# Gated mix of grouped attention and a token-shift MLP: eleven products instead of twelve in the token mixing's w2, one product per group for the maxima, and query splits moved to GpSimd

## The chip, the cores and the metric

The kernel is one program on one core of a Trainium2 chip. The number that counts is the device time of one execution in microseconds (us); the median over several runs is given. The engines named below are PE (TensorE's matrix products; "PEld" is its loading of the stationary operand), DVE (VectorE), ACT (ScalarE), POOL (GpSimd), and SP, which here does nothing but issue transfers (DMAs). Each engine works through its own list of instructions in order, and an instruction that waits holds up all that is behind it on the same engine. The kernel schedules by hand: the order in which the Python code emits instructions is the order on each engine.

## The reference, cut to what matters

```python
x = A_x                                             # [1, 2048, 448]
g = sigmoid((x * gate_w).sum(-1, keepdims=True))
# a: 16 heads of 28, one shared key and value head
q = (x @ wq) per head; k = x @ wk; v = x @ wv
a = softmax(q k^T / sqrt(28)) v, heads joined, @ wo
# b: token mixing, then an MLP
h = gelu(layernorm(x) @ w1)                         # [2048, 448], four quarters of 112 channels
hs = concat(h0 shifted by +1, h1 by -1, h2 by +2, h3 by -2 tokens) @ w2
x1 = x + hs
b = x1 + gelu(layernorm(x1) @ w3) @ w4              # hidden width 1792
out = g * a + (1 - g) * b
```

All of it is float32. The kernel gets near float32 accuracy out of a faster, shorter format (`F32R`) by splitting each operand into a high and a low part, and by summing three products: high·high, high·low, low·high.

## The kernel before, in words

Tokens are worked on in four blocks of 512 (`NB`), each with four tiles of 128. A **unit** `u` is one block of queries with one group of four heads, so there are 16 units (`NU`), and `b, g = divmod(u, 4)`.

**Stage 1** makes queries, keys, values (`stage_q`, results to the DRAM buffer `qd`), and the token mixing. `stage_w1(b)` makes h for a block: for each quarter m (112 channels on partitions 0 to 111), eleven products, a multiplication by the layernorm factor on DVE (L410), two gelus on ACT giving the high part `hh[b]` and an unsplit copy (L411, L412), and the subtraction on POOL that leaves the low part `hl[b]` (L413). At its end POOL copies two columns between neighbouring blocks (L419, L420) or zeroes them (L417, L422). `stage_w2(b)` then needs for each of four tiles t and quarters m the products hh·w2h, hh·w2l and hl·w2h (L429 to L431): twelve products of 112 rows, 128 tokens, 448 columns, added into x1 by DVE (L433). The shift is a column offset in `hh`/`hl`. Rows 112 to 127 of `hh`, `hl`, `w2h` and `w2l` are unused.

The order is w1(0), w1(1), w2(0), w1(2), w2(1), four query products, w1(3), w2(2), w2(3). Between them the SP queue carries, in program order: the layernorm factors on their way through DRAM (`ln1_send` L371, `ln1_read` L376), `stage_kv` (L328, 16 rows of `qd` into `vT`, two transfers per block), `xt_write` (L166), and the loads for the MLP (`load_w34` L556, L557; `xt_read` L171, L173). After tile 0 of w2(2), `stage_v` transposes `vT` on PE (L349), and DVE copies the result out (L351, L352). So the PE's queue stands still there until `vT` of block 3 is loaded.

**Stage 2** is the MLP: for each block b, 14 steps f; a step has eleven products for w3 (`w3_part`, L130 to L134), two gelus (L634, L635), a DVE subtraction (`gl`, L636), and, two steps behind, twelve products for w4 (`w4_part`, L644 to L646). In between lie small jobs. One of them is the softmax's shift: for each unit, the maximum over the first 32 keys (`MK`) of each head's scores. The units 0 to 6 are done in block 2 at steps 2 to 8, the units 7 to 15 in block 3 at steps 0 to 8. In each such step: `max_cast` (DVE rounds the loaded queries into `qh0`, L620; then SP loads those of the next unit, L178), the w4 products, `max_all` (four products with 128 queries as the stationary and the keys `khd` as the moving operand, L203; DVE takes maxima straight out of PSUM, L204), and `max_end` (three small DVE operations, L223 to L227). `max_send` writes the result into `qd` in the next step: eight transfers, four issued by SP and four by ACT (L237).

**Stage 3** is attention: for every unit eight steps v, `k = 8u + v`. A step makes scores for two tiles of 128 keys (L820, four heads side by side on PE), exponentials on ACT (L830), where for head 3 DVE first copies the scores to SBUF (L828) and ACT works on the copy (L835), and then the products with the values of the step before (L845), added by DVE (L850). `q_begin(u)` splits a unit's loaded queries into high and low (`q_split`: L183, L184, on DVE). `q_begin(1)` and the fetch of unit 2 stand ahead of the loop; unit u + 2 follows at v = 6 of unit u.

Of the kernel before, what the change touches and what calls it, by code (L numbers as in the profile page):

```python
# [9 lines left out]
F32 = mybir.dt.float32  # L10
F32R = mybir.dt.float32r
AF = mybir.ActivationFunctionType
ALU = mybir.AluOpType
# [3 lines left out]
P = 128  # L17
# [19 lines left out]
def f32(ap):  # L37
    return ap.bitcast(F32)
# [3 lines left out]
def gated_mix_kernel(  # L42
# [134 lines left out]
        qr_of[u] = raw  # L177
        nc.sync.dma_start(raw, qd[g, :, 512 * b:512 * b + 512])  # L178

    def q_split(u, qh, ql):  # L180
        qr = qr_of.pop(u)
        qh_of[u], ql_of[u] = qh, ql
        nc.vector.tensor_copy(qh, qr)  # L183
        nc.vector.tensor_sub(ql, qr, f32(qh))  # L184

    def score(u, ps, j, keys, first=None, i=None):
        r = 32 * j
# [9 lines left out]
    def max_tile(name):  # L197
        return psA.tile([P, 512], F32, tag="mx", bufs=1, name=name)

    def max_all(u, ps):  # L200
        mx_of[u] = late.tile([P, 4, 4], F32, tag="mr", bufs=1, name=f"mr_{u}")
        for t in range(4):
            nc.tensor.matmul(ps[:, t * P:(t + 1) * P], qh_of[u][:, t * P:(t + 1) * P], khd, start=True, stop=True)  # L203
        nc.vector.reduce_max(mx_of[u].rearrange("p j t -> p t j"), ps.rearrange("p (t j k) -> p t j k", t=4, j=4), axis=AX.X)  # L204

    def max_full(u, tile_of):
        mr = s3.tile([P, 4, 4], F32, tag="mf", bufs=2, name=f"mf_{u}")
        for j in range(4):
            for t in range(4):
                mk = s3.tile([P, NB], F32, tag="mk", bufs=2, name=f"mk_{u}_{j}_{t}")  # L210
                for kb in range(NB):
                    ps = tile_of(f"mf_{u}_{j}_{t}_{kb}")
                    for n, rows, w, a in score(u, ps, j, slice(kb * 512, kb * 512 + 512), DH):
                        nc.tensor.matmul(ps, a[:, t * P:(t + 1) * P], w, start=(n == 0), stop=(n == 2),
                                         tile_position=(32 * j, 0))
                    nc.vector.reduce_max(mk[:, kb:kb + 1], ps, axis=AX.X)
                nc.vector.reduce_max(mr[:, j, t:t + 1], mk, axis=AX.X)
        mx_of[u] = mr

    def max_end(u, again=False):  # L220
        mr = mx_of.pop(u).rearrange("p j t -> p (j t)")
        mc = late.tile([P, 32], F32R, tag="mc", bufs=1, name=f"mc_{u}")
        nc.vector.tensor_scalar(mc[:, 0:16], mr, -1.0, None, op0=ALU.mult)  # L223
        nc.vector.scalar_tensor_tensor(mc[:, 16:32], mr, -1.0, f32(mc)[:, 0:16],
                                       op0=ALU.mult, op1=ALU.subtract)
        mrow = late.tile([P, 32], F32, tag="mrow", bufs=1, name=f"mrow_{u}")
        nc.vector.transpose(mrow, f32(mc))  # L227
        row_of[u] = mrow
        if again:
            max_send(u, f32(qh_of[u]), nc.sync)  # L230

    def max_send(u, q, other):
        mrow = row_of.pop(u)
        for k in range(2):
            for p in range(4):
                r = 32 * p + 16 * k
                (other if k else nc.sync).dma_start(  # L237
                    q[DH + k:P:32, :].rearrange("j (t p q) -> p j t q", p=4, q=32)[p], mrow[r:r + 16, :])

    ctx2 = ExitStack()  # L240

# [1 line left out]
    with tc.tile_pool(name="s1b", bufs=1) as s1b, \  # L243
# [156 lines left out]
        def stage_w1(b, between=None):  # L400
# [14 lines left out]
            for tt in (hh, hl):  # L415
# [5 lines left out]
                if b == NB - 1:  # L421
                    nc.gpsimd.memset(f32(tt[b])[0:C, :, 514:516], 0.0)  # L422

        def stage_w2(b, between=None):
            for t in range(4):
                ps = hs_tile(f"hs_{b}_{t}")[:, 0:D]
                for m in range(4):
                    o = 2 + t * P + SHIFTS[m]
                    nc.tensor.matmul(ps, hh[b][0:C, m, o:o + P], w2h[0:C, m, :], start=(m == 0), stop=False)  # L429
                    nc.tensor.matmul(ps, hh[b][0:C, m, o:o + P], w2l[0:C, m, :], start=False, stop=False)  # L430
                    nc.tensor.matmul(ps, hl[b][0:C, m, o:o + P], w2h[0:C, m, :], start=False, stop=(m == 3))  # L431
                xt = x1[:, 4 * b + t, :]
                nc.vector.tensor_add(xt, xt, ps)  # L433
                if between:
                    between(t)
# [56 lines left out]
                ln1_read(1)  # L492

        stage_w1(0, first)

        def second(m):
            if m < 2:
# [3 lines left out]
                ln1_tile(2, 2 * m - 3)  # L501

        stage_w1(1, second)
        stage_kv(0)
        stage_kv(1)

# [9 lines left out]
        ln1_tile(3, 3)  # L516
        mv0, rs0 = stats_tiles(s1, "m")
        stage_w1(2, lambda t: stats_tile(s1, 0, t, mv0))
        stats_end(mv0, rs0)
        ln1_send(3)  # L520
        ln1_read(3)
# [5 lines left out]
        for u in range(12, 16):  # L527
            stage_q(u)
        stage_w1(3)
        stage_kv(3)  # L530
        s1_stack.close()

# [75 lines left out]
    with tc.tile_pool(name="s2", bufs=1, reuse_waits="tile") as s2, \  # L608
# [3 lines left out]
                nc.gpsimd.tensor_scalar(x1[:, n, :], x1[:, n, :], gi[:, n:n + 1], None, op0=ALU.mult)  # L612

        def max_load(u):
            if u < NU:
                q_load(u, s2a.tile([P, 512], F32, tag="xn", bufs=1, name=f"qm_{u}"))

        def max_cast(u):
            qh_of[u] = qh0
            nc.vector.tensor_copy(qh0, qr_of.pop(u))  # L620
            max_load(u + 1) if u != 6 else None

        def w3_part(b, f):
            i, k = divmod(f, 2)
# [23 lines left out]
        for b in range(NB):  # L648
            acc = [ps2.tile([P, 512], F32, tag="acc", bufs=4, name=f"acc_{b}_{t}") for t in range(4)]
            gs = {}  # L650
            for f in range(NF):
                if f == 9 and b + 1 < NB:
                    mv, rs = layernorm_stats(s2a, b + 1)
                if f == 10 and b + 1 < NB:
                    xt4 = big(f"xt4_{b + 1}")[:, 0:4 * D].rearrange("p (f t j) -> p f t j", f=NE, t=4)
                if f in (10, 11) and b + 1 < NB:
                    for t in (2 * f - 20, 2 * f - 19):
                        xn = s2a.tile([P, 512], F32, tag="xn", bufs=1, name=f"xn_{b + 1}_{t}")[:, 0:D]
                        layernorm_norm(b + 1, t, mv, rs, xn, xt4)
                if f == 11 and b + 1 < NB:  # L660
                    xt_write(b + 1, xt4)
                    ln_read(b + 1)
                gs[f] = w3_part(b, f)
                if b == 0 and f % 2 and f < 11:
                    split_w3((f + 3) // 2)
                    split_w4((f + 3) // 2)
                    if f < 9:
                        load_w34((f + 5) // 2, s2a if f == 1 else s2)
                if b == 1 and f == 0:
                    nc.gpsimd.tensor_tensor(gg, invE, gz, ALU.pow)  # L670
                    nc.vector.tensor_scalar(gg, gg, 1.0, None, op0=ALU.add)
                    nc.vector.reciprocal(gg, gg)
                    nc.vector.tensor_scalar(gi, gg, -1.0, 1.0, op0=ALU.mult, op1=ALU.add)
                if b == NB - 1 and f == 4:
                    weigh_x1(0, 4 * b)
                if b == 1 and f in (0, 2, 4, 6):
                    load_k(f // 2, s2a.tile([P, 512], F32, tag="xn", bufs=1, name=f"kf_{f // 2}"))
                if b == 1 and f in (1, 3, 5, 7):
                    split_k(f // 2)
                if b == 2 and f == 1:  # L680
                    nc.gpsimd.memset(f32(khd), 0.0)
                    for j in range(4):
                        nc.sync.dma_start(f32(khd)[32 * j:32 * j + DH, j, :], f32(kH)[0:DH, 0:MK])
                    max_load(0)
                u = f - 2 if b == 2 and 2 <= f <= 8 else f + 7 if b == 3 and f <= 8 else None
                if b == 2 and f == 12:
                    max_load(7)
                if row_of:
                    w, = row_of
                    max_send(w, qd[w % NG, :, w // NG * 512:w // NG * 512 + 512], nc.scalar)  # L690
                if u is not None:
                    max_cast(u)
                if b == NB - 1 and f == 11:
                    q_load(0, s2a.tile([P, 512], F32, tag="xn", bufs=1, name="qr_0"))
                if b == NB - 1 and f == 13:
                    q_split(0, qh0, ql0)
                if f >= 2:
                    for t in range(4):
                        w4_part(f - 2, t, gs[f - 2], acc)
                if u is not None:  # L700
                    max_all(u, max_tile(f"m_{u}") if u % 2 else misc_tile(f"m_{u}"))
                    max_end(u)
            for t in range(4):
                w4_part(NF - 2, t, gs[NF - 2], acc, NF - 2 if b == NB - 1 else NF - 1)
                if b + 1 < NB:
# [11 lines left out]
    with tc.tile_pool(name="s3", bufs=1, reuse_waits="tile") as s3, \  # L717
# [18 lines left out]

        def q_begin(u):
            q_split(u, s3.tile([P, 512], F32R, tag="qh", bufs=3, name=f"qh_{u}"),
                    s3.tile([P, 512], F32R, tag="ql", bufs=3, name=f"ql_{u}"))

        q_fetch(1)
        q_begin(1)
        q_fetch(2)

        on_of = {}

# [112 lines left out]

        for k in range(NU * NV):  # L860
            u, v = divmod(k, NV)
            if v == 6 and u + 2 < NU:
                q_begin(u + 2)
                q_fetch(u + 3)
# [106 lines left out]
        with tc.If(again > 0, label="redo"):  # L971
            for b in range(NB):
                for g in range(NG):
# [1 line left out]
                    q_fetch(u)  # L975
                    q_begin(u)
                    max_full(u, bank)
                    max_end(u, True)
                    pv = take()
                    for kt in range(NT):  # L980
                        for j in range(4):
# [64 lines left out]
```

## Time and profile before

| | us |
|---|---|
| median of 3 runs (956.57 to 958.59) | 956.84 |
| the profiled execution | 957.32 |
| its span in the trace | 955.5 |
| PE busy | 928.2 |
| ACT busy | 645.6 |
| DVE busy | 549.2 |
| POOL busy | 74.5 |

Stage 1 fills the span up to 128.65 us, the MLP up to some 420 us, attention the rest. The shares of busy time are means over these stages, so what a change is worth has to be read from the stage in which it lies. In rows of the timeline the columns are start, duration (of the merged run of x instructions), engine, line, operation, tile, and in brackets the engine's idle time before it with what ended it. "SPq" rows are the issuing of transfers, not the transfers. In rows of windows, each engine has its busy time and count, and behind them stands the clock that PE was granted (1.00 is full), the share of the DMA engines' time, and GB/s.

### The profile page before, as it was taken

How to read it: one execution, taken by the hardware profiler on the slowest of the kernel's cores; microseconds unless marked ns; L12 is line 12 of the kernel's file. 1: busy time of each engine (PE TensorE's matmuls, PEld its weight loads, DVE VectorE, ACT ScalarE, POOL GpSimd, SP SyncE). 2: the span in 40 equal slices, each digit the busy share in tenths (PEclk: the TensorE clock that was granted, in tenths of full speed). 3: DMA queues.
4: the chain of work that ended last, by engine and by line, in shares of the span. 5: the costliest groups of instructions: out<-in, count | busy, mean ns of one | idle time of the engine just before them, and what ended most of it. 6: DMA issues, size and time to landing. Idle time of an engine off the chain costs nothing. (4 is left out here: it accounts for less than half of the span.)

```text
span 955.5 us, 24595 instructions
## 1 busy us (share of the span) xinstructions
PE 928.2 (97%) x10099; PEld 651.6 (68%) x10099; DVE 549.2 (57%) x1095; ACT 645.6 (68%) x1262; POOL 74.5 (8%) x105
## 2 busy tenths in 40 slices
PE   9999999999999989979999999999999999999996
PEld 6788888888888868865555555555555555555553
DVE  4664254532444544336667776776777767776674
ACT  5442444232321221138999999999999999999994
POOL 2232200221000520020000000000000000000000
PEclk9999999999999989989999999999999999999999
DMA  9802452210311311110000001100010000010001
GB/s 305 283 29 50 131 165 84 70 38 14 90 28 48 79 39 48 36 60 3 25 14 24 14 25 43 34 14 25 14 45 33 25 14 24 24 54 2 14 14 43
DMA packets 41079, 50.75 MB, mean 53 GB/s; under 512 B 9136, under 2 KB 27264, under 8 KB 40960
## 3 DMA queue, kind: packets, MB, share of 16 engines
q1 hardware_dynamic: 36656, 43.52, 15.6%
q10 hardware_dynamic: 4304, 5.61, 1.7%
q8 instruction: 80, 1.31, 0.6%
q14 instruction: 39, 0.32, 0.1%
HBM read 37.04 MB, written 11.93 MB: 51 GB/s over the span
## 5 line engine op out<-in xcount | busy, mean ns | idle before, releaser
L830 ACT ACTIVATE p<-bank 128x512 f32<-128x512 f32 x768 | 391.4, 628 | 9.1 <-PE bank L820 7.4
L845 PE MATMUL bank<-p,vext 128*32 128x256 f32 x4096 | 247.0, 382 | 2.1 <-ACT p L830 1.7
L828 DVE COPY p<-bank 128x512 f32<-128x512 f32 x256 | 175.1, 690 | 45.5 <-PE bank L820 44.7
L845 PEld LDWEIGHTS bank<-p,vext 128*32 128x32 f32 x4096 | 131.1, 110 | 91.9 <-DVE p L828 6.9
L634 ACT ACTIVATE gh<-g 128x512 fp32r<-128x512 f32 x55 | 32.8, 597 | 204.0 <-PE g L134 199.6
L835 ACT ACTIVATE p<-p 128x512 f32<-128x512 f32 x256 | 154.2, 687 | 3.4 <-DVE p L828 3.4
L850 DVE TENSOR_TENSOR o<-o,bank 128x256 f32<-128x256 f32 x222 | 93.5, 421 | 93.1 <-PE bank L845 49.2
L820 PE MATMUL bank<-qh,kH 30*128 30x512 f32 x1024 | 119.0, 445 | 5.3 <-DVE p L828 5.3
L636 DVE TENSOR_TENSOR gl<-gf,gh 128x512 fp32r<-128x512 f32 x55 | 38.6, 702 | 134.4 <-ACT gf L635 134.4
L820 PE MATMUL bank<-qh,kL 28*128 28x512 f32 x1024 | 106.1, 393 | 0.0
L820 PE MATMUL bank<-ql,kH 28*128 28x512 f32 x1024 | 105.4, 390 | 0.0
L820 PEld LDWEIGHTS bank<-qh,kH 30*128 30x128 f32 x1024 | 60.9, 183 | 63.4 <-ACT p L830 51.8
L645 PE MATMUL acc<-w4l,gh 128*128 128x448 f32 x220 | 80.4, 366 | 0.0
L644 PE MATMUL acc<-w4h,gh 128*128 128x448 f32 x220 | 80.3, 365 | 0.0
L646 PE MATMUL acc<-w4h,gl 128*128 128x448 f32 x220 | 80.2, 365 | 0.0
L782 PE MATMUL bank<-wof,on 128*32 128x224 f32 (+1 forms) x992 | 73.1, 370 | 5.2 <-ACT p L830 0.4
L130 PE MATMUL g<-ah,w3h 128*128 128x512 f32 x168 | 67.8, 403 | 0.0
L131 PE MATMUL g<-al,w3h 128*128 128x512 f32 x168 | 66.8, 397 | 0.0
L132 PE MATMUL g<-ah,w3l 128*128 128x512 f32 x168 | 66.4, 395 | 0.0
L782 PEld LDWEIGHTS bank<-wof,on 128*32 128x32 f32 x992 | 20.0, 108 | 56.7 <-ACT p L830 55.3
L820 PEld LDWEIGHTS bank<-ql,kH 28*128 28x128 f32 x1024 | 52.6, 186 | 8.7
L820 PEld LDWEIGHTS bank<-qh,kL 28*128 28x128 f32 x1024 | 52.0, 186 | 0.1
(188 smaller groups left out, 1083.4 us busy)
## 6 DMA issues: line engine op xcount, KB each, us to landing
qd<-qf ACTq DMA_DIRECT2D x16, 256.0 KB
qm<-qd SPq DMA_DIRECT2D x16, 256.0 KB
qr<-qd SPq DMA_DIRECT2D x16, 256.0 KB
rb<-rd SPq DMA_DIRECT2D x15, 256.0 KB
x<-in_x_dram SPq DMA_DIRECT2D x4, 896.0 KB
xd<-xt SPq DMA_DIRECT2D x16, 224.0 KB
w34raw<-in_w_dram SPq DMA_DIRECT2D x7, 512.0 KB
out_dram<-ot SPq DMA_DIRECT2D x15, 224.0 KB
```

Source lines behind the costliest of these rows:

```text
L130: nc.tensor.matmul(ps, wh[:, c, :], ah[:, c, :], start=(c == 0), stop=False)
L131: nc.tensor.matmul(ps, wh[:, c, :], al[:, c, :], start=False, stop=False)
L644: nc.tensor.matmul(ps, gh[:, tok], w4h[i][:, k, :], start=(f == 0), stop=False)
L645: nc.tensor.matmul(ps, gh[:, tok], w4l[i][:, k, :], start=False, stop=False)
L646: nc.tensor.matmul(ps, gl[:, tok], w4h[i][:, k, :], start=False, stop=(f == stop))
L782: nc.tensor.matmul(ps[32 * j:32 * j + 32, cols], on_of[u][:, tok], wof[:, g, cols], start=True, stop=True, tile_position=(0, 32 * j))
L820: nc.tensor.matmul(bs[j], w, a, start=(i == 0), stop=(i == 2), tile_position=(32 * j, 0))
L828: nc.vector.tensor_copy(ps[j], bs[j])
L830: nc.scalar.activation(ps[j], bs[j], AF.Exp, scale=SCALE)
L835: nc.scalar.activation(p_of[u, kt][j], p_of[u, kt][j], AF.Exp, scale=SCALE)
L845: nc.tensor.matmul(pv[32 * j:32 * j + 32, q], vext[:, kt, :], p_of[u, kt][j][:, q], start=(kt % 2 == 0), stop=(kt % 2 == 1), tile_position ...
L850: nc.vector.tensor_add(o_of[u][:, q], o_of[u][:, q], pv[:, q])
```

## The change

Four edits come together.

1. **w2.** The product hl·w2h of quarter m = 2 is dropped. Its 112 rows are cut into seven pieces of 16, and each piece is copied into rows 112 to 127 of the operands of seven other products, which now run with 128 rows: hh·w2l for m = 0, 1, 3, 2 and hl·w2h for m = 0, 1, 3. The copies are transfers from SBUF to SBUF on SP: `carry_w2` (seven, once) and `carry_h(b)` (seven per block). `carry_w2` and `carry_h(0)` are emitted behind w1(0), the others behind w1(1), w1(2) and w1(3), each ahead of what SP had there.
2. **Maxima.** `max_first` makes one product per unit with the keys stationary and 512 queries moving. DVE transposes the result in blocks of 32 x 32 from PSUM to SBUF, and takes the maxima there. The rounded queries alternate between `qh0` and `ql0`, and the product for unit u comes one step f later than its cast. `max_send` is four transfers on SP.
3. **Query splits** in attention run on POOL instead of DVE.
4. `q_begin(1)` and `q_fetch(2)` move from ahead of the loop into it, at k = 3.

```diff
+    def max_first(u, q, ps, mt):
+        nc.tensor.matmul(ps, khd.rearrange("p j k -> p (j k)"), q, start=True, stop=True)
+        mt = mt.rearrange("p (t k) -> p t k", k=MK)
+        nc.vector.transpose(mt, ps.rearrange("p (t q) -> p t q", q=32))
+        mx_of[u] = late.tile([P, 16], F32, tag="mr", bufs=1, name=f"mr_{u}")
+        nc.vector.reduce_max(mx_of[u], mt, axis=AX.X)
...
+    def max_send(u):
+        mrow = row_of.pop(u)
+        b, g = divmod(u, NG)
+        for j in range(4):
+            nc.sync.dma_start(qd[g, 32 * j + DH:32 * j + DH + 2, 512 * b:512 * b + 512].rearrange("k (t q) -> k t q", q=32),
+                              mrow[32 * j:32 * j + 32, :])
...
+        CARRY = [(0, 0, w2l), (0, 1, w2l), (0, 3, w2l), (0, 2, w2l), (1, 0, w2h), (1, 1, w2h), (1, 3, w2h)]
+
+        def carry_w2():
+            for i, (_, m, w) in enumerate(CARRY):
+                nc.sync.dma_start(f32(w)[C:P, m, :], f32(w2h)[16 * i:16 * i + 16, 2, :])
+
+        def carry_h(b):
+            for i, (low, m, _) in enumerate(CARRY):
+                o = 2 + SHIFTS[m]
+                nc.sync.dma_start(f32((hl if low else hh)[b])[C:P, m, o:o + 512], f32(hl[b])[16 * i:16 * i + 16, 2, 0:512])
...
-                    nc.tensor.matmul(ps, hh[b][0:C, m, o:o + P], w2l[0:C, m, :], start=False, stop=False)
-                    nc.tensor.matmul(ps, hl[b][0:C, m, o:o + P], w2h[0:C, m, :], start=False, stop=(m == 3))
+                    nc.tensor.matmul(ps, hh[b][:, m, o:o + P], w2l[:, m, :], start=False, stop=False)
+                    if m != 2:
+                        nc.tensor.matmul(ps, hl[b][:, m, o:o + P], w2h[:, m, :], start=False, stop=(m == 3))
...
         stage_w1(0, first)
+        carry_w2()
+        carry_h(0)
...
         stage_w1(1, second)
+        carry_h(1)
         stage_kv(0)
         stage_kv(1)
...
         stage_w1(2, lambda t: stats_tile(s1, 0, t, mv0))
+        carry_h(2)
         stats_end(mv0, rs0)
         ln1_send(3)
...
         stage_w1(3)
+        carry_h(3)
         stage_kv(3)
...
-            qh_of[u] = qh0
-            nc.vector.tensor_copy(qh0, qr_of.pop(u))
-            max_load(u + 1) if u != 6 else None
+            qm_of[u] = (qh0, ql0)[u % 2]
+            nc.vector.tensor_copy(qm_of[u], qr_of.pop(u))
...
+                if row_of:
+                    max_send(*row_of)
+                u = M_AT.get(b * NF + f)
+                if u is not None:
+                    max_cast(u)
+                    if u not in (6, 15):
+                        max_load(u + 1)
...
-                if u is not None:
-                    max_all(u, max_tile(f"m_{u}") if u % 2 else misc_tile(f"m_{u}"))
-                    max_end(u)
+                for w in tuple(qm_of):
+                    if w != u:
+                        max_first(w, qm_of.pop(w), max_tile(f"m_{w}") if w % 2 else misc_tile(f"m_{w}"),
+                                  big(f"mt_{w}")[:, 0:512])
+                        max_end(w)
...
             q_split(u, s3.tile([P, 512], F32R, tag="qh", bufs=3, name=f"qh_{u}"),
-                    s3.tile([P, 512], F32R, tag="ql", bufs=3, name=f"ql_{u}"))
+                    s3.tile([P, 512], F32R, tag="ql", bufs=3, name=f"ql_{u}"), nc.gpsimd)
 
         q_fetch(1)
-        q_begin(1)
-        q_fetch(2)
...
             u, v = divmod(k, NV)
+            if k == 3:
+                q_begin(1)
+                q_fetch(2)
```

The fallback branch behind the kernel's end (`redo`, not taken in the profiled execution) is adapted to the new helpers.

More of the change, by code (lines that the diff above doesn't have):

```diff
@@ L178, in q_load, with q_split @@
         nc.sync.dma_start(raw, qd[g, :, 512 * b:512 * b + 512])
-    def q_split(u, qh, ql):
+    def q_split(u, qh, ql, engine):
         qr = qr_of.pop(u)
         qh_of[u], ql_of[u] = qh, ql
-        nc.vector.tensor_copy(qh, qr)
-        nc.vector.tensor_sub(ql, qr, f32(qh))
+        engine.tensor_copy(qh, qr)
+        engine.tensor_tensor(ql, qr, f32(qh), ALU.subtract)
     def score(u, ps, j, keys, first=None, i=None):
@@ L198, in max_tile @@
         return psA.tile([P, 512], F32, tag="mx", bufs=1, name=name)
[L200 to L204, printed above, removed]
+    def max_first(u, q, ps, mt):
[4 more added lines that the diff above has]
+        nc.vector.reduce_max(mx_of[u], mt, axis=AX.X)
     def max_full(u, tile_of):
@@ L217, in max_full, with max_end @@
                 nc.vector.reduce_max(mr[:, j, t:t + 1], mk, axis=AX.X)
-        mx_of[u] = mr
-    def max_end(u, again=False):
-        mr = mx_of.pop(u).rearrange("p j t -> p (j t)")
+        mx_of[u] = mr.rearrange("p j t -> p (j t)")
+    def max_end(u):
+        mr = mx_of.pop(u)
         mc = late.tile([P, 32], F32R, tag="mc", bufs=1, name=f"mc_{u}")
@@ L228, in max_end, with max_set @@
         row_of[u] = mrow
-        if again:
-            max_send(u, f32(qh_of[u]), nc.sync)
-    def max_send(u, q, other):
+    def max_send(u):
[4 more added lines that the diff above has]
+                              mrow[32 * j:32 * j + 32, :])
+    def max_set(u):
         mrow = row_of.pop(u)
@@ L236, in max_send @@
                 r = 32 * p + 16 * k
-                (other if k else nc.sync).dma_start(
-                    q[DH + k:P:32, :].rearrange("j (t p q) -> p j t q", p=4, q=32)[p], mrow[r:r + 16, :])
+                nc.sync.dma_start(
+                    f32(qh_of[u])[DH + k:P:32, :].rearrange("j (t p q) -> p j t q", p=4, q=32)[p], mrow[r:r + 16, :])
     ctx2 = ExitStack()
@@ L614, in max_load @@
         def max_load(u):
-            if u < NU:
-                q_load(u, s2a.tile([P, 512], F32, tag="xn", bufs=1, name=f"qm_{u}"))
+            q_load(u, s2a.tile([P, 512], F32, tag="xn", bufs=1, name=f"qm_{u}"))
+        qm_of = {}
         def max_cast(u):
-            qh_of[u] = qh0
-            nc.vector.tensor_copy(qh0, qr_of.pop(u))
-            max_load(u + 1) if u != 6 else None
+            qm_of[u] = (qh0, ql0)[u % 2]
+            nc.vector.tensor_copy(qm_of[u], qr_of.pop(u))
+        M_AT = {2 * NF + f: f - 2 for f in range(2, 9)}
+        M_AT.update({3 * NF + f: f + 7 for f in range(9)})
         def w3_part(b, f):
@@ L684, in gated_mix_kernel @@
                     max_load(0)
-                u = f - 2 if b == 2 and 2 <= f <= 8 else f + 7 if b == 3 and f <= 8 else None
+                if row_of:
[5 more added lines that the diff above has]
+                        max_load(u + 1)
                 if b == 2 and f == 12:
                     max_load(7)
-                if row_of:
-                    w, = row_of
-                    max_send(w, qd[w % NG, :, w // NG * 512:w // NG * 512 + 512], nc.scalar)
-                if u is not None:
-                    max_cast(u)
                 if b == NB - 1 and f == 11:
@@ L695, in gated_mix_kernel @@
                 if b == NB - 1 and f == 13:
-                    q_split(0, qh0, ql0)
+                    q_split(0, qh0, ql0, nc.vector)
                 if f >= 2:
@@ L699, in gated_mix_kernel @@
                         w4_part(f - 2, t, gs[f - 2], acc)
-                if u is not None:
-                    max_all(u, max_tile(f"m_{u}") if u % 2 else misc_tile(f"m_{u}"))
-                    max_end(u)
+                for w in tuple(qm_of):
[3 more added lines that the diff above has]
+                        max_end(w)
             for t in range(4):
@@ L977, in gated_mix_kernel @@
                     max_full(u, bank)
-                    max_end(u, True)
+                    max_end(u)
+                    max_set(u)
                     pv = take()
```

## The prediction

> **What bounds the kernel now.** I read the page first, then the waits of all engines, then each stage in windows, and last the timeline of each place that the change touches. PE is busy for nearly the whole span, but its clock and its real idle time show only in windows:
>
> ```profile
> PE 928.2 (97%) x10099; PEld 651.6 (68%) x10099; DVE 549.2 (57%) x1095; ACT 645.6 (68%) x1262; POOL 74.5 (8%) x105
> ```
>
> ```profile
> 108.50:118.70 10.20, 10.20 (x53) 9.39 (x52) 4.39 (x8) 5.83 (x10) 3.65 (x12) 1.00 0.18 51
> ...
> 346.10:349.90 3.80, 3.80 (x13) 3.02 (x12) 1.26 (x4) 0.00 (x0) 0.00 (x0) 0.61 0.27 70
> ...
> 353.40:357.20 3.80, 3.80 (x14) 3.06 (x14) 1.25 (x4) 0.00 (x0) 0.00 (x0) 0.67 0.26 70
> ...
> 428.20:432.50 4.30, 4.29 (x39) 2.59 (x43) 1.94 (x3) 4.23 (x9) 0.00 (x0) 0.50 0.25 61
> ...
> 461.00:948.00 487.00, 479.97 (x7749) 281.63 (x7745) 340.18 (x688) 478.59 (x965) 0.48 (x1) 1.00 0.08 24
> ```
>
> In token mixing (108.5 to 118.7, w2 of block 2) PE is busy in every microsecond: there a product removed is time gained, and a wait added is time lost. In attention from 461 on ACT is busy 478.59 of 487.00 us and sets the pace, with PE close behind. The three short windows are places where PE had just stood idle: it worked on with 0.61, 0.67 and 0.50 of its clock.
>
> **w2: products removed.** Twelve products per tile become eleven; 112 or 128 rows make no difference to the pace.
>
> ```profile
> 108.48 0.37 PE L429 MATMUL hs<-w2h,hh 112*128 112x448 f32 x1
> ...
> 110.73 0.36 PE L431 MATMUL hs<-w2h,hl 112*128 112x448 f32 x1
> 110.93 0.60 PE L349 MATMUL vp<-ident,vT 128*128 128x128 f32 x4
> ```
>
> From the first product of a tile to the twelfth is 2.25 us over eleven steps, 0.205 each. 16 tiles x 0.205 = **-3.3 us**.
>
> **w2: the copies on SP.** 35 transfers are new, all on SP, so I price an issue and a landing. No such copy is in the trace. The nearest are the pieces of `kf`: 12 or 16 rows of 2 KB, eight in a run, with POOL waiting for the last.
>
> ```profile
> 220.84 5.70 SPq L338 DMA_DIRECT2D kf<-qd  x8
> ```
>
> ```profile
> 228.82 0.61 POOL L343 CAST kH<-kf 128x512 fp32r<-128x512 f32 x1 [8.00 <-DMA kf<-qd]
> ```
>
> 5.70 / 8 = 0.71 us per issue, and 228.82 - 226.54 = 2.28 us from the last issue's end to the data. Ends for the range:
>
> ```profile
> 66.10 0.26 SPq L371 DMA_DIRECT2D rsd<-rT  x1
> 67.30 0.31 SPq L376 DMA_DIRECT2D rsb<-rsd  x1
> ```
>
> ```profile
> 257.21 3.34 SPq L683 DMA_DIRECT2D khd<-kH  x4
> ...
> 276.83 0.34 SPq L178 DMA_DIRECT2D qm<-qd  x1
> ```
>
> A lone issue takes 0.34 us; four SBUF-to-SBUF copies took 3.34, 0.84 each; the quickest landing is 67.30 - 66.36 = 0.94.
>
> *First place, w2(0).* `carry_w2` and `carry_h(0)` start where SP was free for `stage_kv`, at 51.17:
>
> ```profile
> 51.17 2.83 SPq L328 DMA_DIRECT2D vT<-qd  x4
> ```
>
> ```profile
> 58.59 0.36 PE L431 MATMUL hs<-w2h,hl 112*128 112x448 f32 x1
> ```
>
> The first copy into `hl` is the twelfth of the fourteen: 51.17 + 12 x 0.71 + 2.28 = 61.97. PE wants it for its third product at 58.59: **+3.4** (low: 12 x 0.34 + 0.94, in time, 0; high: 12 x 0.84 + 2.28, 4.9). The two later `hl` copies come 0.7 us apart, about as PE reaches them. PE loses clock too: 3.80 us at 0.61 is a loss of 1.5, at 0.67 of 1.3; I take **+1.4** (0 without the stall, at most 2.2, from 4.30 at 0.50).
>
> *Second place, `stage_v`.* This is the largest term. `carry_h(3)` stands ahead of `stage_kv(3)` on SP. Its source includes the two columns that POOL copies last:
>
> ```profile
> 112.25 0.20 POOL L419 CAST hl<-hl 112x8 fp32r<-112x8 f32 x1
> ```
>
> ```profile
> 99.15 3.02 SPq L328 DMA_DIRECT2D vT<-qd  x2
> ```
>
> So SP stands until 112.45, where before `vT` was fetched at 99.15. Then come seven copies and two pieces of `vT`: 112.45 + 9 x 0.71 + 2.28 = 121.1. PE reaches the transposes of `vT`, which before began at 110.93, at 110.73 with eleven products, and all of w2(2) and w2(3) is queued behind them: **+10.4** (low 9 x 0.34 + 0.94: 5.8; high 9 x 0.84 + 2.28: 11.6). Clock behind it: **+1.8** (1.3 to 2.2). Both places shift POOL and PE alike, so neither eats the other. Behind the same wait on SP lie the loads of weights and `xr`, but their readers lie behind the stall as well.
>
> The Trainium skill, "TensorE: Matmul & The Clock Gate", in its section on why this matters, asks for no PE gaps over about 3 us. By it the first stall's longest gap of 2.7 us would cost no clock, and the sum would be 1.4 lower. The rows below disagree: gaps of 2.40 and 2.33 us were enough.
>
> `carry_h(1)` and `carry_h(2)` delay `ln1_read` by some 3 us. Cost 0: stage_w1 has four PSUM tiles, so PE runs on, and DVE has the next stage to catch up. Without that cover it would be some 3 us each.
>
> Token mixing: -3.3 + 3.4 + 1.4 + 10.4 + 1.8 = **+13.7** (+3.8 to +17.6).
>
> **Maxima.** The page of the MLP is PE alone, so I read the period of a step from ACT's first gelu, with and without maxima:
>
> ```profile
> 280.27 0.60 ACT L634 ACTIVATE gh<-g 128x512 fp32r<-128x512 f32 x1 [4.53 <-PE g L134]
> ...
> 296.80 0.60 ACT L634 ACTIVATE gh<-g 128x512 fp32r<-128x512 f32 x1 [4.43 <-PE g L134]
> ...
> 401.16 0.60 ACT L634 ACTIVATE gh<-g 128x512 fp32r<-128x512 f32 x1 [3.85 <-PE g L134]
> ...
> 411.04 0.60 ACT L634 ACTIVATE gh<-g 128x512 fp32r<-128x512 f32 x1 [3.85 <-PE g L134]
> ```
>
> 16.53 / 3 = 5.51 with, 9.88 / 2 = 4.94 without: 0.57 per unit. The steps 0 and 1 of block 3 have no w4 products that cover the cast:
>
> ```profile
> 269.25 0.39 PE L134 MATMUL g<-ah,w3l 128*128 128x512 f32 x1
> ...
> 274.23 0.39 PE L134 MATMUL g<-ah,w3l 128*128 128x512 f32 x1
> ...
> 342.67 0.39 PE L134 MATMUL g<-ah,w3l 128*128 128x512 f32 x1
> 345.46 0.89 PE L203 MATMUL m<-khd,qh 128*128 128x128 f32 x4 [2.40 <-DVE qh L620]
> ...
> 352.59 1.08 PE L203 MATMUL m<-khd,qh 128*128 128x128 f32 x4 [2.33 <-DVE qh L620]
> ...
> 356.96 0.40 PE L134 MATMUL g<-ah,w3l 128*128 128x512 f32 x1
> ```
>
> PE waits there for DVE's cast, then runs slow: 14.29 us from 342.67 to 356.96 for two steps, which in block 2 took 4.98 without maxima. After the change the cast is a step old, and a product of 512 columns costs 2.49 / 11 = 0.23. The two steps then need 4.98 + 0.23 = 5.21 (-9.1). The other 14 maxima cost 14 x 0.57 before, the other 15 cost 15 x 0.23 now (-4.5). Together **-13.6**. DVE's transpose of 512 columns is new, some 0.7 us by `xt` (646 ns for 448 columns):
>
> ```profile
> 281.39 0.69 DVE L636 TENSOR_TENSOR gl<-gf,gh 128x512 fp32r<-128x512 f32 x1 [2.35 <-ACT gf L635]
> ...
> 344.82 0.49 DVE L620 CAST qh<-qm 128x512 fp32r<-128x512 f32 x1
> ```
>
> ```profile
> L159 DVE STREAM_TRANSPOSE xt<-xn 128x448 f32<-128x448 f32 x16 | 10.3, 646 | 0.6
> ...
> L344 POOL TENSOR_TENSOR kL<-kf,kH 128x512 fp32r<-128x512 f32 x4 | 5.2, 1288 | 0.3
> ...
> L343 POOL CAST kH<-kf 128x512 fp32r<-128x512 f32 x4 | 2.4, 610 | 39.7 <-DMA kf<-qd 39.7
> ```
>
> DVE idles 2.35 us per step: cost 0. It would count only if `gl` came later than the two steps that w4 leaves it. Four transfers fewer sit on ACT, which is far from the bound here. Bounds: if the cast of unit 7 is still late in step 1 (DVE ended it at 345.3, PE now arrives at 345.4), one wait with its clock stays, 2.4 + 1.5: -9.7. Upper end -14.5.
>
> **Attention's start.**
>
> ```profile
> 426.41 0.43 DVE L183 CAST qh<-qr 128x512 fp32r<-128x512 f32 x1 [4.95 <-DMA qr<-qd]
> ```
>
> ```profile
> 428.21 0.80 PE L820 MATMUL bank<-qh,kH 30*128 30x512 f32 x3 [5.33 <-DVE p L828]
> ```
>
> ```profile
> 428.19 1.23 ACT L835 ACTIVATE p<-p 128x512 f32<-128x512 f32 x2 [3.42 <-DVE p L828]
> ...
> 435.57 3.05 ACT L830 ACTIVATE p<-bank 128x512 f32<-128x512 f32 x6 [2.00 <-PE bank L820]
> ```
>
> DVE stood at unit 1's cast for 4.95 us with the copies of scores behind it; PE lost 5.33, ACT 3.42. With the cast gone the copies follow the scores, and ACT, the bound, gains 3.4. Its next gap of 2.00 comes from the slow clock at 428.2; I take 1.5 of it. **-4.9** (-3.4 to -5.4). On POOL unit 1's split takes 0.61 + 1.29 by the rows of `kH` and `kL`, is ready by some 429, and is wanted a unit later, near 456.
>
> **Splits on POOL.** From 461 ACT has no gap, so DVE's relief is worth 0. POOL is idle and units ahead: 0. SP's fetches wait for POOL instead of DVE, no later.
>
> **Sum.** 13.7 - 13.6 - 4.9 = -4.8 against the profiled execution's 957.3: 952.5. The median of the runs shown lies 0.5 below that execution, so 952.0. The ends: 3.8 - 14.5 - 5.4 = -16.1 (940.7), 17.6 - 9.7 - 3.4 = +4.5 (961.3).
>
> **The rivals.**
>
> *Cheap copies.* At 0.34 us per issue and 0.94 to land, token mixing costs 3.8: 957.3 + 3.8 - 13.6 - 4.9, less 0.5, 942. For it: small lone issues. Against: runs of issues all show 0.6 and more.
>
> *Dear copies: slower.* Each further 0.1 us per copy adds 1.2 at w2(0) and 0.7 at `stage_v`. It turns slower by 2 us at +0.36, 1.07 per copy; at 1.2 it gives 961. For it: the SBUF-to-SBUF copies are the dearest, 0.84. Against: nothing near 1.07.
>
> *Late cast.* One wait stays in block 3: 956.
>
> *Attention's start keeps its stall*, another wait taking its place, such as the banks: 957. Against: the waits name only DVE's copy.
>
> *POOL blocks DVE.* If a split (0.61 + 1.29 us) stopped DVE and so ACT, 14 x 1.9 = +26.6: 978. Against:
>
> ```profile
> 419.02 2.44 DVE L713 TENSOR_TENSOR x<-x,acc 128x448 f32<-128x448 f32 x4 [0.17 <-PE acc L646]
> ```
>
> ```profile
> 419.74 5.55 POOL L612 TENSOR_SCALAR x<-x,gi 128x448 f32<-128x448 f32 x4 [23.31 <-DVE x L713]
> ```
>
> 2.44 / 4 = 0.61 each, with POOL at work beside them. The Trainium skill, "SBUF — State Buffer", calls the pair of ports that DVE and GpSimd share an exclusive lock; this row shows no sign of it.
>
> **How the numbers follow.** Likeliest 0.57 (its own range 947 to 957); cheap copies 0.15; dear copies 0.12; late cast 0.07; start keeps its stall 0.06; POOL 0.03. A measurement tells 0.2%, 1.9 us, from no change. Faster: 0.57 less its upper tail, cheap copies, and a part of late cast: 0.73. Same 0.08. Slower: dear copies, POOL and tails, 0.19. The range 942 to 960 leaves out the far ends.
>
> **What would show it.** PE idle near 10 us ahead of the transposes of `vT`, waiting for a transfer; some 3 us at w2(0); no wait on a cast in block 3's first steps, and a step of 5.17 with maxima; ACT's first 3.4 us gap gone; no new ACT gaps behind 461. I am wrong if `vT` arrives in time, or if ACT waits where POOL splits.

## The result, and the profile after

The changed kernel takes 949.39 us (median of 5, 948.19 to 952.07) against 958.59 for the kernel before measured beside it (956.57 to 959.77). The ratio is 0.9913, with a 95% interval from 0.9890 to 0.9937: faster by 0.6 to 1.1%. In the profiled executions the span fell from 955.5 to 946.5 us, 9.0, where 4.8 was forecast. The page of the changed kernel:

```profile
span 946.5 us, 24485 instructions
...
PE 916.2 (97%) x10035; PEld 646.1 (68%) x10035; DVE 546.6 (58%) x1081; ACT 644.4 (68%) x1262; POOL 103.8 (11%) x135
```

That share of PE hides what happened: one stage lost, two gained. PE's timeline of the changed kernel in token mixing, with the idle time in brackets:

```profile
60.97 0.44 PE L449 MATMUL hs<-w2h,hl 128*128 128x448 f32 x1 [1.46 <-POOL hl L419]
...
88.01 0.48 PE L446 MATMUL hs<-w2h,hh 112*128 112x448 f32 x1 [1.05 <-DVE x L451]
...
122.44 1.09 PE L355 MATMUL vp<-ident,vT 128*128 128x128 f32 x4 [9.51 <-DMA vT<-qd]
```

The transposes of `vT` (L355 now) wait 9.51 us for a transfer. The first row's releaser is not the true one: POOL had ended at 54.9, and the product also waits for the first copy into `hl`. SP's rows show when that copy was issued (the first four), and what the transfer at 122.44 was waiting for (the last three):

```profile
51.87 2.54 SPq L434 DMA_DIRECT2D w2l<-w2h  x4
54.46 1.86 SPq L434 DMA_DIRECT2D w2h<-w2h  x3
56.41 2.43 SPq L439 DMA_DIRECT2D hh<-hl  x4
58.89 1.85 SPq L439 DMA_DIRECT2D hl<-hl  x3
...
114.50 2.75 SPq L439 DMA_DIRECT2D hh<-hl  x4
117.36 1.78 SPq L439 DMA_DIRECT2D hl<-hl  x3
119.18 1.37 SPq L334 DMA_DIRECT2D vT<-qd  x2
```

SP stood until POOL's small copy into the columns that it reads had ended (114.47), issued seven copies, then the two pieces of `vT`, which landed 1.9 us after the last issue's end. Windows over that wait and behind it, with the granted clock in the third column from the right:

```profile
112.80:122.40 9.60, 0.14 (x1) 0.00 (x0) 0.62 (x1) 0.07 (x1) 2.74 (x11) 0.72 0.16 38
122.40:126.20 3.80, 3.76 (x12) 3.48 (x13) 0.72 (x2) 0.00 (x0) 0.00 (x0) 0.50 0.96 301
126.20:132.50 6.30, 6.30 (x30) 5.75 (x30) 2.19 (x4) 1.60 (x4) 0.00 (x0) 0.92 0.41 134
```

PE idles for the wait and then works at half its clock. The MLP's first product comes at 140.9 us instead of 128.7:

```profile
L130 PE MATMUL g<-ah,w3h x168: 388/389/397, 140.9 to 413.0; 128*128 128x512 f32 x168
```

In the MLP the waits on DVE's cast are gone. ACT's first gelus of steps 0, 1, 2 and 3 of block 3:

```profile
352.67 0.60 ACT L660 ACTIVATE gh<-g 128x512 fp32r<-128x512 f32 x1 [5.37 <-PE g L134]
...
355.16 0.60 ACT L660 ACTIVATE gh<-g 128x512 fp32r<-128x512 f32 x1 [1.41 <-PE g L134]
...
358.12 0.60 ACT L660 ACTIVATE gh<-g 128x512 fp32r<-128x512 f32 x1 [1.86 <-PE g L134]
...
363.29 0.60 ACT L660 ACTIVATE gh<-g 128x512 fp32r<-128x512 f32 x1 [4.09 <-PE g L134]
```

The two steps take 358.12 - 352.67 = 5.45 us, where they took 14.29, and the next, with w4 and a maximum, 5.17. At attention's start ACT idles for 0.86 us, where before it idled for 3.42 and 2.00:

```profile
420.08 3.04 ACT L857 ACTIVATE p<-bank 128x512 f32<-128x512 f32 x6 [3.37 <-PE bank L847]
422.96 1.19 ACT L862 ACTIVATE p<-p 128x512 f32<-128x512 f32 x2
...
428.97 3.05 ACT L857 ACTIVATE p<-bank 128x512 f32<-128x512 f32 x6 [0.86 <-PE bank L847]
```

PE's clock was at 0.50 from 424.2 to 427.6 there, ahead of those 0.86 us (the last section shows it).

The span splits at the MLP's first product and at attention's first exponential (421.73 before, 420.08 after):

| stage | before | after | change | forecast |
|---|---|---|---|---|
| up to the MLP | 128.7 | 140.9 | +12.2 | +13.7 |
| MLP | 293.0 | 279.2 | -13.8 | -13.6 |
| attention | 533.8 | 526.4 | -7.4 | -4.9 |
| span | 955.5 | 946.5 | -9.0 | -4.8 |

Some 0.8 of the first row is not the change's: w2(0) began at 58.94 instead of 58.17, ahead of anything changed, and over the experiments it began between 57.46 and 59.73. Token mixing proper lost 11.5.

### The profile page after: what moved, and what is told of

Same layout as the page of the kernel before. It is cut to its first block, busy times and chain, and to the rows that moved or that the text cites. A ratio compares the mean times of both kernels' runs of the same rounds, so it can differ in the third digit from the quotient of the medians.

```text
span 946.5 us, 24485 instructions
## 1 busy us (share of the span) xinstructions
PE 916.2 (97%) x10035; PEld 646.1 (68%) x10035; DVE 546.6 (58%) x1081; ACT 644.4 (68%) x1262; POOL 103.8 (11%) x135
## 5 line engine op out<-in xcount | busy, mean ns | idle before, releaser
L847 PEld LDWEIGHTS bank<-qh,kH 30*128 30x128 f32 x1024 | 60.7, 182 | 58.2 <-ACT p L857 46.5
L670 PE MATMUL acc<-w4h,gh 128*128 128x448 f32 x220 | 80.3, 365 | 0.0
L130 PE MATMUL g<-ah,w3h 128*128 128x512 f32 x168 | 65.6, 390 | 0.0
```

What stands on the lines that cost most here:

```text
L130: nc.tensor.matmul(ps, wh[:, c, :], ah[:, c, :], start=(c == 0), stop=False)
L670: nc.tensor.matmul(ps, gh[:, tok], w4h[i][:, k, :], start=(f == 0), stop=False)
L847: nc.tensor.matmul(bs[j], w, a, start=(i == 0), stop=(i == 2), tile_position=(32 * j, 0))
```

## The experiments

Open after the result: whether the loss really hangs on SP's queue and how far it goes, what made the clock slow, which part of the maxima's edit carries its gain, and why attention gained more than forecast. Ratios are to the kernel before, run beside each.

**w2 alone.** The kernel before with the w2 edit and nothing else:

```diff
+                nc.sync.dma_start(f32(w)[C:P, m, :], f32(w2h)[16 * i:16 * i + 16, 2, :])
...
+        carry_w2()
+        carry_h(0)
...
         stage_w1(3)
+        carry_h(3)
         stage_kv(3)
```

> The kernel before with the w2 edit alone (eleven products, the copies on SP in the changed kernel's places). If the three edits add up as the traces read, it costs what token mixing lost in the changed kernel's trace, 12.25 us less the 0.8 that the start varied: some +11.5 us, near 969. If the loss there had been only an effect of the other edits (it could have been their loads or code), it would be near the kernel before, 957 to 959, or faster by the 3.3 us of products saved.

969.59 us, ratio 1.0116 (1.0084 to 1.0149). Its PE waits 9.46 us at the same place:

```profile
122.45 1.09 PE L349 MATMUL vp<-ident,vT 128*128 128x128 f32 x4 [9.46 <-DMA vT<-qd]
```

Alone, the edit that removes products makes the kernel slower by 11 to 12 us; the other edits carried it.

**The fetch of `vT` first.**

```diff
-        carry_h(3)
         stage_kv(3)
+        carry_h(3)
```

> The changed kernel with the two fetches of vT for block 3 ahead of the seven copies. PE should no longer wait at the transposes of vT. Theory one, the queue position of vT alone costs the time: 9.5 us of wait and some 2.5 of slow clock go, 937.5. Theory two, everything behind the copies on SP is late, and the next to be late is xr (ACT got it at 130.9 in the changed kernel's trace, 18.0 us idle): DVE's addition of tile 3 of w2(2) stands behind ln_split, so PE waits some 10 us in w2(3) instead, and the gain is 1 to 2 us, 947 to 949.

946.5 us, ratio 0.9885 (0.9862 to 0.9908): 2.9 less than the changed kernel, of 12 that were there. In the profiles the stretch from w2(0)'s first product to the MLP's first takes 137.8 - 57.5 = 80.3 us against 140.9 - 58.94 = 82.0, so 1.7 come from the new order. The second theory holds. PE's timeline and ACT's in this run:

```profile
128.40 0.74 PE L446 MATMUL hs<-w2h,hh 112*128 112x448 f32 x1 [7.27 <-DVE x L451]
```

```profile
125.87 2.18 ACT L603 CAST ah<-xr 128x512 fp32r<-128x512 f32 x4 [14.29 <-DMA xr<-xd]
```

`vT` is in time, and PE waits 7.27 us four tiles later, ahead of tile 1 of w2(3). DVE's addition that frees the PSUM tile stands behind `ln_split`, which waits for `xr`, and `xr` is loaded behind the copies and behind the 960 KB of weights that SP issues first. One wait was taken out, and the next on the same queue took its place.

**All loads first.**

```diff
-        carry_h(3)
         stage_kv(3)
...
         xt_read(0, xraw2[0])
+        carry_h(3)
```

> The changed kernel with vT, the first weights of the MLP and xr all ahead of the copies of block 3. Both theories of the run before: 937.5, if nothing else is late; the copy into hl for w2(3) lands near 119.8, about when PE wants it. If instead the copies themselves (their traffic or their landing) hold PE, w2(3) would wait some microseconds and the time be 941 or more.

936.55 us, ratio 0.9779 (0.9757 to 0.9802). PE has no wait left there; a window of this run:

```profile
112.00:134.00 22.00, 22.00 (x109) 19.77 (x108) 13.46 (x25) 8.80 (x16) 3.31 (x13) 1.00 0.41 122
```

Full clock, busy throughout. The copies' own traffic costs nothing that shows.

**Keeping PE busy over the wait.** The changed kernel with products of zeros written into the tile that the transposes overwrite; the output is unaffected.

```diff
             vp = misc_tile("vp")
+            for _ in range(72):
+                nc.tensor.matmul(vp[:, 0:256], warm[:, 0:P], warm, start=True, stop=True)
```

> The changed kernel with 72 products of zeros (bf16, 128x256, some 0.11 us each) ahead of the transposes of vT, which keep PE busy for about 8 of the 9.5 us that it waits. If the slow clock behind the wait comes from PE having been idle, the products behind it run at full pace and 2 to 2.5 us are gained: 947. If it has another cause: 949.4, as the changed kernel, or more.

945.62 us, ratio 0.9879 (0.9854 to 0.9904), 3.8 below the changed kernel. In the profiles, from w2(0)'s first product to the MLP's first it is 137.5 - 57.46 = 80.0 us against 140.9 - 58.94 = 82.0. Of the 4.5 us between the two spans, 1.5 are the varying start, and 1.0 is attention, 525.4 us against 526.4, where this run has no slow clock at the start. PE's rows and a window of this run:

```profile
111.44 8.04 PE L355 MATMUL vp<-warm 128*128 128x256 bf16 x72
121.24 0.63 PE L357 MATMUL vp<-ident,vT 128*128 128x128 f32 x4 [1.76 <-DMA vT<-qd]
```

```profile
122.40:126.20 3.80, 3.80 (x20) 3.52 (x19) 0.84 (x3) 0.00 (x0) 0.00 (x0) 1.00 1.05 387
```

The wait for `vT` is as late as it was, PE idles only for its last 1.76 us, and the clock behind it is 1.00 instead of 0.50. So the slow clock behind this wait came from the idling, and was worth 2.0 us.

**Everything ahead that can be.** The loads first, and besides:

```diff
+            if m == 0:
+                carry_w2()
             if m == 2:
                 ln1_send(1)
...
         stage_w1(0, first)
-        carry_w2()
         carry_h(0)
...
-        carry_h(1)
         stage_kv(0)
         stage_kv(1)
+        carry_h(1)
```

> The run with the loads first, and in addition the seven copies of w2 issued in w1(0) as soon as their source is there, and the fetches of vT for blocks 0 and 1 ahead of the copies of block 1. If the two short waits left in token mixing are queue positions too (1.65 us at the first low product of w2(0), 1.15 in w2(1) behind a late layernorm factor), they go, but for some 0.5 us in w2(0), where the copies still start only when POOL ends: 934.3. If the landing of the copies or another load sets them, 936.5.

933.98 us, ratio 0.9745 (0.9729 to 0.9761), the fastest of all. Its window from w2(0)'s first product to the MLP's first:

```profile
59.70:127.20 67.50, 67.49 (x315) 57.09 (x314) 33.78 (x69) 22.33 (x38) 18.23 (x35) 1.00 0.35 99
```

67.5 us without a gap, where the kernel before took 128.7 - 58.2 = 70.5. Here the 16 products removed pay their 3 us; in the changed kernel this stretch takes 82.0.

**Maxima a step later, in their old form.**

```diff
-            qh_of[u] = qh0
-            nc.vector.tensor_copy(qh0, qr_of.pop(u))
+            qh_of[u] = (qh0, ql0)[u % 2]
+            pend.append(u)
+            nc.vector.tensor_copy(qh_of[u], qr_of.pop(u))
...
+                for w in tuple(pend):
+                    if w != u:
+                        pend.remove(w)
+                        max_all(w, max_tile(f"m_{w}") if w % 2 else misc_tile(f"m_{w}"))
+                        max_end(w)
```

> The kernel before with the maxima's products one step later than the cast, and the cast queries alternating between two tiles, but with the four products, DVE's maxima and the eight transfers as they were. If the cover for the cast in steps 0 and 1 of block 3 is most of that edit's gain: 14.29 us become 4.98 + 0.57, -8.7, 948.8 to 949. If the gain comes from the form of the product: -1 at most, 956.5.

948.53 us, ratio 0.9902 (0.9887 to 0.9917), some 9.4 below the kernel before: the delay by a step carries most of that edit's gain. PE's rows of steps 0 to 2 of block 3 in this run:

```profile
343.23 0.39 PE L134 MATMUL g<-ah,w3l 128*128 128x512 f32 x1
...
345.72 0.39 PE L134 MATMUL g<-ah,w3l 128*128 128x512 f32 x1
...
348.80 0.39 PE L134 MATMUL g<-ah,w3l 128*128 128x512 f32 x1
```

5.57 us for the two steps, against 14.29. The remaining 4 to 5 of the MLP's 13.8 belong, by subtraction, to the rest of that edit: one product in place of four, the transpose, and four transfers in place of eight. None of these was tried alone.

**Only unit 1 later, all on DVE.** The kernel before with:

```diff
         q_fetch(1)
-        q_begin(1)
-        q_fetch(2)
...
+            if k == 3:
+                q_begin(1)
+                q_fetch(2)
```

> The kernel before with only the split of unit 1 and the fetch of unit 2 moved into the loop, at k = 3, all splits still on DVE. If the stall at attention's start was DVE's cast in front of its copies: -4.5 us (3.4 of ACT's gap and 1.1 of the next), 953. If another wait takes its place: 957.5.

952.78 us, ratio 0.9943 (0.9927 to 0.9960): 5.2 less. The stall at attention's start was the cast, and no other wait took its place.

**Splits back on DVE.** The changed kernel with:

```diff
-                    s3.tile([P, 512], F32R, tag="ql", bufs=3, name=f"ql_{u}"), nc.gpsimd)
+                    s3.tile([P, 512], F32R, tag="ql", bufs=3, name=f"ql_{u}"), nc.vector)
```

> The changed kernel with all splits of queries back on DVE, at the changed places. My prediction gave POOL's taking them 0: 949.4. The traces say otherwise: of eight steps of a unit before, one took 4.20 us where the others took 3.96, and after the change none does; if that is DVE's split at v = 6, 14 x 0.24 = 3.4 us come back: 952.8.

952.6 us, ratio 0.9950 (0.9935 to 0.9965): 3.2 more than the changed kernel. The two intervals just meet (the changed kernel's ends at 0.9937), so the profiles have to bear it out: attention takes 529.2 us in this run and 526.4 in the changed kernel. ACT's first exponentials of successive steps, in this run and then in the changed kernel:

```profile
633.62 3.04 ACT L857 ACTIVATE p<-bank 128x512 f32<-128x512 f32 x6
...
637.57 3.06 ACT L857 ACTIVATE p<-bank 128x512 f32<-128x512 f32 x6
640.44 1.21 ACT L862 ACTIVATE p<-p 128x512 f32<-128x512 f32 x2
641.76 3.05 ACT L857 ACTIVATE p<-bank 128x512 f32<-128x512 f32 x6
...
645.71 3.05 ACT L857 ACTIVATE p<-bank 128x512 f32<-128x512 f32 x6
```

```profile
636.72 3.05 ACT L857 ACTIVATE p<-bank 128x512 f32<-128x512 f32 x6
...
640.69 3.04 ACT L857 ACTIVATE p<-bank 128x512 f32<-128x512 f32 x6
...
644.65 3.05 ACT L857 ACTIVATE p<-bank 128x512 f32<-128x512 f32 x6
```

Steps of 3.95, 4.19, 3.95 us here, 3.97 and 3.96 there. One step per unit is 0.24 longer, right behind the split, which DVE ran at 637.05 in this run:

```profile
637.05 0.42 DVE L183 CAST qh<-qr 128x512 fp32r<-128x512 f32 x1
637.50 0.69 DVE L184 TENSOR_TENSOR ql<-qr,qh 128x512 fp32r<-128x512 f32 x1
```

No row lists this as idle time of ACT: its work before ends at 640.44 + 1.21 = 641.65, 0.11 us ahead of the next step, so the loss stands only in the period. Where it comes from shows in the waits of PE's weight loads for the products with the values (total us, times, longest), in this run and then in the changed kernel:

```profile
PEld bank L872 <- DVE p L855: 7.2, 17, 0.5
```

```profile
PEld bank L872 <- DVE p L855: 0.9, 3, 0.3
```

With the splits on DVE there are 14 more of them, as many as there are splits at v = 6. They wait for DVE's copy of the scores of head 3, which stands behind the split.

## Why the prediction was right, and where it was not

The direction and the range held. The size was half of what was measured: 4.8 forecast in the span, 9.0 found.

- *Products removed, -3.3.* The rows bear it out: 70.5 us became 67.5 where no wait was in the way.
- *First place, w2(0), +3.4 and +1.4 of clock.* Oversized. PE waited 1.46 us, and lost no clock. An issue took 0.61 to 0.64 instead of the 0.71 taken from `kf`, and the copy was there 1.46 us after its issue ended (59.51 to 60.97) instead of 2.28. The row I chose for both was a fetch from DRAM; a copy between places in SBUF landed sooner.
- *Second place, `stage_v`, +10.4 and +1.8.* Right in mechanism and nearly in size: 9.5 and 2.0. (The low end of its range is 5.7 by its own terms, not 5.8; nothing hangs on it.) I said that the loads behind the same wait cost nothing, as their readers lie behind the stall. That was so in the changed kernel, but it also meant that the stall could not be mended by moving `vT` alone, as the run with `vT` first shows.
- *"Cost 0" for the late layernorm factor.* Wrong by 1.05 us: DVE caught up too late for the PSUM tile that PE wanted in w2(1). The run with everything ahead removed it.
- *Maxima, -13.6.* Measured -13.8, and the delay carries some 9 of it, as the working had it.
- *Attention's start, -4.9.* Measured alone 5.2. In the changed kernel the first unit takes 34.4 us (420.08 to 454.43, ACT's first exponentials of units 0 and 1) where it took 39.3 (421.73 to 460.99), 4.9 less. That it fits so closely is luck in part: in the run with products of zeros that unit takes 33.4, so the slow clock, which is in no term of the sum, took 1.0 us back.
- *Splits on POOL, 0.* This is the step that failed. I read "From 461 ACT has no gap" as if ACT were never held up. PE follows ACT closely there, and DVE's 1.1 us of split at v = 6 delays its copies, for which PE then waits (by the kernel's code a copy's end returns a PSUM tile to PE). The sum over 14 units is 3.2 us in the times, 2.8 in the profiles.

Of the 4.2 us between forecast and result, the table of stages puts 2.5 in attention, about what the splits were worth. Another 1.5 lie ahead of the MLP: 2.2 were forecast too much there, and the varying start took 0.8 of it back. Those 2.2 are a balance, too: w2(0) was forecast 3.3 too dear, and the late factor's 1.05 was not forecast at all.

Of the rivals, *cheap copies* was right in direction at w2(0) alone. *POOL blocks DVE* fell: with the splits on POOL the steps of units 3 to 13 take 3.95 to 3.98 us, and DVE's copies of scores 691 ns, 690 before. So the exclusive lock that the Trainium skill describes ("SBUF — State Buffer") did not show in the time. But the run hardly tests the lock: those copies take their input from PSUM, as did one input of the additions (`x<-x,acc`) by which I had set the rival aside, and DVE's multiplications with both inputs in SBUF (`on<-o,rb`, 684 ns) never ran beside a split.

## What to carry to other kernels

A transfer that waits for fresh data blocks whatever is issued behind it on the same queue. Before adding one, list what stands behind it with the time at which each is wanted, and put the waiting transfer behind all that is ready; mending only the first late load exposes the next. Where an engine seems gapless, compare the period of its steps, since many small delays show in no idle row.

## What the runs showed of the hardware

The 0.61 and 0.67 of the prediction are averages over windows that hold both full clock and half. With other edges, the kernel before shows 0.50 behind its waits of 2.40 us (until 345.46) and 2.33 us (until 352.59), and 1.00 between:

```profile
345.70:349.00 3.30, 3.30 (x11) 2.72 (x11) 1.26 (x4) 0.00 (x0) 0.00 (x0) 0.50 0.30 79
349.20:352.40 3.20, 1.06 (x5) 0.54 (x3) 0.98 (x2) 1.09 (x2) 0.00 (x0) 1.00 0.02 3
352.60:355.90 3.30, 3.30 (x10) 2.82 (x11) 1.25 (x4) 0.00 (x0) 0.00 (x0) 0.50 0.30 81
```

These runs give no length of wait at which the clock falls. One of 1.76 us left it at 1.00 (the run with products of zeros). But in the run with w2 alone one of 2.89 us left it at 1.00 as well, and the next, of 2.33 us, was followed by 0.50. PE's rows there, and windows behind each wait:

```profile
358.57 0.63 PE L203 MATMUL m<-khd,qh 128*128 128x128 f32 x4 [2.89 <-DVE qh L637]
...
364.09 1.09 PE L203 MATMUL m<-khd,qh 128*128 128x128 f32 x4 [2.33 <-DVE qh L637]
```

```profile
358.50:361.70 3.20, 3.13 (x15) 2.43 (x15) 1.25 (x4) 0.00 (x0) 0.00 (x0) 1.00 0.31 82
364.00:367.30 3.30, 3.21 (x10) 2.76 (x11) 1.08 (x4) 0.00 (x0) 0.00 (x0) 0.50 0.34 81
```

At attention's start the clock of the changed kernel fell with no wait above 0.55 us ahead of it. The run with products of zeros has the same wait at the same place and went on at full clock, with 1.93 us for the products that took 3.35. A window and PE's row of the changed kernel, then the row of the run with products of zeros:

```profile
424.20:427.60 3.40, 2.91 (x28) 1.38 (x32) 1.10 (x2) 3.40 (x8) 1.42 (x2) 0.50 0.02 5
```

```profile
424.69 3.35 PE L872 MATMUL bank<-p,vext 128*32 128x256 f32 x32 [0.55 <-ACT p L857]
```

```profile
421.18 1.93 PE L874 MATMUL bank<-p,vext 128*32 128x256 f32 x32 [0.55 <-ACT p L859]
```

Why it fell in the one and not in the other stays open. The clock gate's rule of some 3 us in the Trainium skill ("TensorE: Matmul & The Clock Gate", why this matters) is no safe limit for this kernel, since waits shorter than that were followed by half the clock. Its advice to leave PE no longer gaps than that was worth 2.0 us at the wait of 9.5 us, where it was tried.
